# A decode layer on one core: where the hand-written section of all engines ends, and how w_down's loads are issued

## The chip, the core and the metric

One core of one Trainium2 chip runs the whole kernel. The metric is device time in microseconds, the median of the runs; a profiled execution stands beside it with a trace of every instruction and of every DMA packet. TensorE (PE), VectorE (DVE), ScalarE (ACT) and GpSimd (POOL) compute; SyncE (SP) issues nearly all loads. All loads share sixteen DMA engines.

## What is computed

One token goes through an attention block with a cached context of 65,536 positions and a gated feed-forward block, in bf16:

```python
x = A_x                                   # 1 x 1 x 1024
h = x + attention(layernorm(x), k_cache, v_cache, wq, wo)   # 32 query heads, 4 kv heads, Sk = 65536, Dh = 128
g = gelu(layernorm(h) @ w_gate)           # w_gate 1024 x 3584
u = layernorm(h) @ w_up                   # w_up   1024 x 3584
out = h + (g * u) @ w_down                # w_down 3584 x 1024
```

The caches are 134 MB and the weights 39 MB; each byte is read once and used for a single token.

## The kernel before

**Loads.** All weights and caches pass through `ring`, a buffer of four slots of 32 KB in each of 128 partitions. SP issues the loads in program order: wq, the K and V chunks in a loop over eight half-heads, wo in two halves, then `w_gate` (7168 KB, slots 0 and 1, issued when the last product with V has been taken out of them), `w_up` (7168 KB, slots 2 and 3, when wo has been used), and `w_down` in six pieces:

- wa, 4096 KB, into slot 0, and wb, 2048 KB, into slot 1, both once gate's matmuls are done with these slots;
- 768 KB into `w_end`, a buffer of its own outside of the ring, and
- the last 256 KB, also into `w_end`, in three loads over 57 odd partitions, 7 odd partitions and the 64 even ones.

**Order of the work.** Two mechanisms set it. `Flow` is a list written out by hand: each `op` or `dma` names what it reads and writes, and `Flow.issue` (lines 83 to 118) emits the instructions in list order with the least waits on the kernel's own semaphores. Its output stands in a *critical section* (line 612): to the framework's scheduler the section is one unit, which begins through SP and ends in a join. At the end every engine that took part drains and signals; SP waits for all signals and then signals the end, and only behind that come instructions that depend on the section. A second section (line 658) holds the first part of the down projection. Outside of sections the scheduler places the semaphores itself, from what each instruction reads and writes; `manual_schedule` makes it keep TensorE's instructions in the order written, and `keep_in_program_order` does so for single instructions of SP.

**The feed-forward part.** `ffn_in` loads a matrix, multiplies it in eight steps (`wide_rows`, four matmuls side by side into each of the banks 0 and 1) and brings the rows into columns by two DVE transposes. For gate that is followed by the gelu on DVE and ACT (`t1`, `th`, `hg`, `gl`). The residual h is put into the output's accumulators `d_ps` (bank 2) and `d_odd` (bank 7) by eight matmuls against `hb`, which POOL fills by a memset and a product; POOL also clears `actz`, into whose column the product of gate and up is written. Then the down projection: `stay_busy(4)` runs four filler matmuls, `down_wide` takes wa's part in 32 matmuls of 512 columns, ACT copies the result to `e_sb`, `stay_busy(3)` fills, `add_wide` folds it into the accumulators, and `down` takes wb's 8 rows and `w_end`'s 3 + 1 rows in 8 matmuls of 128 columns each. DVE and ACT take the two halves of the accumulators to bf16, and SP stores them.

**Names and lines.** Everything that `Flow.issue` emits has line 105 in the profile (waits of its own: 101). L172: the first load. L612: the first section's begin and end. L621: the loads into `w_end`. L631: `down`. L638: `stay_busy`. L646: `down_wide`. L653: `add_wide`. L658: the second section's begin and end. L665: `e_sb`. L673: waits on `w_end`'s loads. L677 to L679: the output. In the profile `ktb` stands for whatever lies over that buffer at the time, `hb`, `actz`, the transposed rows and `at_r` among them.

In the kernel before, the first section ends behind the product of gate and up:

```python
    u_r = ffn_in(B_w_up, "u_r", 2, 0)
    op("dve", "tensor_tensor", r=["u_r0", "u_r1", "gl", "actz"], w=["actz"], out=actz[:, :, AZ], in0=u_r, in1=gl[:], op=ALU.mult)
```

Of the kernel before, what the change touches and what calls it, by code (L numbers as in the profile page):

```python
# [8 lines left out]
ACT = mybir.ActivationFunctionType  # L9
ALU = mybir.AluOpType  # L10
# [108 lines left out]
def kernel(  # L119
# [13 lines left out]
    nc = tc.nc  # L133
    P = 128
    D = A_x.shape[-1]
# [4 lines left out]
    F = B_w_gate.shape[1]  # L140
    DC = D // P
    FC = F // P
# [39 lines left out]
    def sb(name, shape, dtype=F32):  # L182
        return const.tile(shape, dtype, name=name)
# [22 lines left out]
    def slot(i, n=1):  # L206
        return ring[:, i * CW:(i + n) * CW]
# [5 lines left out]
    act_go = tc.alloc_semaphore("to_act")  # L213
    STEPS = 4
    k_sem = [tc.alloc_semaphore("k_landed_%d" % i) for i in range(DCH)]
    end_sem = [tc.alloc_semaphore("end_landed_%d" % i) for i in range(2)]


    XU = 32
# [333 lines left out]
    def f_blocks(w_row):  # L553

        blocks = []
        for o, n in zip((0, P * FA), FW):
            blocks += [w_row[:, o + q * n:o + (q + 1) * n] for q in range(4)]
        return blocks

    def ffn_in(wmat, key, s0, b0):  # L560
        banks = [bank[b0 + i][:, 0:n] for i, n in enumerate(FW)]
        bkeys = ["B%d" % (b0 + i) for i in range(2)]
# [3 lines left out]
        for ci in range(DC):  # L566
            wide_rows(banks, bkeys, hz, "xz", ci, f_blocks(wv[:, ci, :]), rk, ci == 0, ci == DC - 1)
        return rows_to_columns(banks, bkeys, key, "p (j e) -> p e j", j=32)

    g_sb = ffn_in(B_w_gate, "g_r", 0, 0)  # L570
    t1 = sb("t1", [P, FC])
    op("dve", "tensor_tensor", r=["g_r0", "g_r1"], w=["t1"], out=t1[:], in0=g_sb, in1=g_sb, op=ALU.mult)
    op("dve", "tensor_scalar", r=["t1"], w=["t1"], out=t1[:], in0=t1[:], scalar1=0.044715, scalar2=1.0, op0=ALU.mult, op1=ALU.add)
    op("dve", "tensor_tensor", r=["t1", "g_r0", "g_r1"], w=["t1"], out=t1[:], in0=t1[:], in1=g_sb, op=ALU.mult)
    th = sb("th", [P, FC])
    op("act", "activation", r=["t1"], w=["th"], out=th[:], in_=t1[:], func=ACT.Tanh, scale=0.7978845608028654)
    hg = sb("hg", [P, FC])
    op("dve", "tensor_scalar", r=["g_r0", "g_r1"], w=["hg"], out=hg[:], in0=g_sb, scalar1=0.5, scalar2=None, op0=ALU.mult)
    gl = sb("gl", [P, FC])
    op("dve", "scalar_tensor_tensor", r=["th", "hg"], w=["gl"], out=gl[:], in0=th[:], scalar=1.0, in1=hg[:], op0=ALU.add, op1=ALU.mult)  # L580


    OR = 8
    OB = D // OR
    orow = [30, 94, 31, 95, 32, 96, 33, 97]
    d_ps = bank[2][:, 0:OB]
    op("dve", "memset", w=["B2"], ap=d_ps, constant=0.0)
    hb = over(10240, [DC, P])
    op("pool", "memset", w=["hb"], ap=hb, constant=0.0)
    op("pool", "tensor_tensor", r=["h_col", "o_of"], w=["hb"], out=hb.rearrange("p j (b m) -> p j m b", b=2)[:, :, orow[0]:orow[0] + OR // 2, :],  # L590
       in0=h_col[:].unsqueeze(2).unsqueeze(3).to_broadcast([P, DC, OR // 2, 2]),
       in1=o_of[:].rearrange("p (a b) -> p a b", b=2).unsqueeze(1).to_broadcast([P, DC, OR // 2, 2]), op=ALU.mult)
    for j in range(DC):
        op("pe", "matmul", r=["hb", "sel16"], w=["B2"], out=d_ps[:, j:OB:DC], lhsT=hb[:, j, :], rhs=sel16[:],
           start=False, stop=False, skip_group_check=True)
    d_odd = bank[7][:, 0:OB]
    op("dve", "tensor_copy", r=["B2"], w=["B7"], out=d_odd[64:P, :], in_=d_ps[64:P, :])

    AZ = 31
    actz = over(16384, [FC, 2 * AZ + 2], BF16)  # L600
    op("pool", "memset", w=["actz"], ap=actz, constant=0.0)
    u_r = ffn_in(B_w_up, "u_r", 2, 0)
    op("dve", "tensor_tensor", r=["u_r0", "u_r1", "gl", "actz"], w=["actz"], out=actz[:, :, AZ], in0=u_r, in1=gl[:], op=ALU.mult)

    wa = slot(0)[:, 0:FA * D].rearrange("p (e n) -> p e n", e=FA)
    wb = slot(1)[:, 0:FB * D].rearrange("p (e n) -> p e n", e=FB)
    parts = [(wa, 0, FA, f.dma("sp", wa, B_w_down[0:P * FA, :].rearrange("(p e) n -> p e n", p=P), after=["R0"], inc=(r_sem[0], 16)), r_sem[0])]
    e0 = 0
    w_body = wb_src[:, e0:FB - FZ, :]
    part = wb[:, e0:FB - FZ, :]  # L610
    parts.append((part, FA + e0, FB - FZ - e0, f.dma("sp", part, w_body, after=["R1"], inc=(r_sem[1], 16)), r_sem[1]))
    with tc.tile_critical(no_gpsimd_drain=True):  # L612
        f.issue()

    ends = []
    odd = [57, 7]
    for i, (e1, e2, rows) in enumerate(((FB - FZ, FB - 1, [slice(0, P)]),
                                        (FB - 1, FB, [slice(1, 2 * odd[0], 2), slice(2 * odd[0] + 1, P, 2), slice(0, P, 2)]))):
        loads = []
        for p in rows:  # L620
            d = nc.sync.dma_start(out=w_end[p, e1 - FB + FZ:e2 - FB + FZ, :], in_=wb_src[p, e1:e2, :])  # L621
            d.then_inc(end_sem[i], 16)
            tc.no_tile_sem_insts.add(d.ins.name)
            tc.keep_in_program_order(d)
            loads.append(d)
        ends.append((loads, e1, e2))

    def down(a_row, w_row, landed=()):
        for j in (0, 4, 1, 5, 2, 6, 3, 7):
            q, m = divmod(orow[j], 32)  # L630
            mm = nc.tensor.matmul((d_ps, d_odd)[q // 2][32 * q:32 * q + 32, :], lhsT=a_row[:, AZ - m:AZ - m + 32], rhs=w_row[:, j * OB:(j + 1) * OB],  # L631
                             start=False, stop=False, skip_group_check=True, tile_position=(0, 32 * q))
            for d in landed:
                tc.declare_no_dep(mm.ins, d.ins, query=mybir.DependencyQuery.ANY, reason="TensorE waits for the load's own semaphore ahead of it")

    def stay_busy(n):
        for i in range(n):
# [5 lines left out]
    def down_wide(a_row, w_row, e, n):  # L643
        for h in range(DS):
            q = 2 * (e % 2) + h
            mm = nc.tensor.matmul(e_ps[32 * q:32 * q + 32, :], lhsT=a_row[:, AZ:AZ + 32], rhs=w_row[:, h * NB:(h + 1) * NB],  # L646
                             start=(e < 2), stop=(e >= n - 2), tile_position=(0, 32 * q))
        return mm

    def add_wide():  # L650
        for c in range(C4):
# [4 lines left out]
    (w_rows, a0, n, at, sem), (w_rows2, a2, n2, at2, sem2) = parts  # L656
    ctx.enter_context(tc.manual_schedule(engines={mybir.EngineType.PE}))
    with tc.tile_critical(no_gpsimd_drain=True):  # L658
        stay_busy(4)
        nc.tensor.wait_ge(sem, at)  # L660
        for e in range(n):
            mm = down_wide(actz[:, a0 + e, :], w_rows[:, e, :], e, n)
        mm.then_inc(s_step, 1)
        nc.scalar.wait_ge(s_step, STEPS * NT2 + 1)
        nc.scalar.copy(out=e_sb[:], in_=e_ps[:]).then_inc(from_act, 1)  # L665
        stay_busy(3)
        nc.tensor.wait_ge(from_act, 1)
        add_wide()
        nc.tensor.wait_ge(sem2, at2)
        for e in range(n2):  # L670
            down(actz[:, a2 + e, :], w_rows2[:, e, :])
    for i, (d, e1, e2) in enumerate(ends):
        nc.tensor.wait_ge(end_sem[i], 16 * len(d))  # L673
        for e in range(e1, e2):
            down(actz[:, FA + e, :], w_end[:, e - FB + FZ, :], d)
    h2 = sb("h2", [P, 2, OB], BF16)
    nc.vector.tensor_copy(out=h2[0:64, 0, :], in_=d_ps[0:64, :])  # L677
    nc.scalar.copy(out=h2[0:64, 1, :], in_=d_odd[64:P, :])  # L678
# [31 lines left out]
```

## Time and profile before

| | |
|---|---|
| median of 3 runs | 409.45 us (409.44, 409.45, 410.83) |
| profiled execution | 409.35 us |
| its span, first to last instruction | 407.6 us |
| bytes read | 173.02 MB, 424 GB/s over the span |
| busy share of PE, DVE, ACT, POOL | 55%, 49%, 10%, 4% |
| mean granted PE clock | 0.812 of full speed |
| `w_gate` landed, its matmuls done | 370.67, 375.36 us |
| `w_up` landed, its matmuls done | 387.62, 392.30 us |
| wa, wb landed | 397.32, 402.21 us |
| last 32 matmuls of the down projection | 404.44 to 405.07 us |

Times in the trace are counted from the first instruction, so that the span's end is 407.6. A landing is the time at which the last of the sixteen DMA engines has posted its completion of that load; single engines can be far ahead of it. Waits are put down to what released them: "SPq L612 <- DVEq L612" is SP standing in the join until DVE had drained. The granted clock is the share of full speed that TensorE was allowed. Line and operation names of DMA issues (DMA_DIRECT2D) stand on the queue that issues them, SPq.

### The profile page before, as it was taken

How to read it: one execution, taken by the hardware profiler on the slowest of the kernel's cores; microseconds unless marked ns; L12 is line 12 of the kernel's file. 1: busy time of each engine (PE TensorE's matmuls, PEld its weight loads, DVE VectorE, ACT ScalarE, POOL GpSimd, SP SyncE). 2: the span in 40 equal slices, each digit the busy share in tenths (PEclk: the TensorE clock that was granted, in tenths of full speed). 3: DMA queues.
4: the chain of work that ended last, by engine and by line, in shares of the span. 5: the costliest groups of instructions: out<-in, count | busy, mean ns of one | idle time of the engine just before them, and what ended most of it. 6: DMA issues, size and time to landing. Idle time of an engine off the chain costs nothing. (4 is left out here: it accounts for less than half of the span.)

```text
span 407.6 us, 3816 instructions
## 1 busy us (share of the span) xinstructions
PE 225.4 (55%) x1557; PEld 99.4 (24%) x1558; DVE 201.1 (49%) x160; ACT 40.2 (10%) x143; POOL 14.7 (4%) x25
## 2 busy tenths in 40 slices
PE   0432854674677458715971785468467745624156
PEld 0110322231232133203320332223123223222123
DVE  4126860894089328734763686088508940121010
ACT  1000003000300120030003000300030003000000
POOL 4010000001000000010000001000000000030000
PEclk9995996899569778978796889589956986866688
DMA  8999999999999999999998999999999999999995
GB/s 360 412 447 426 447 428 412 460 418 435 431 460 418 412 447 473 412 415 415 489 431 383 444 421 450 418 463 412 415 453 463 418 412 418 461 450 435 394 413 219
DMA packets 4967, 173.10 MB, mean 425 GB/s; under 512 B 606, under 2 KB 610, under 8 KB 866
## 3 DMA queue, kind: packets, MB, share of 16 engines
q1 hardware_dynamic: 4914, 173.02, 98.6%
q8 instruction: 4, 0.07, 0.1%
q10 hardware_dynamic: 48, 0.00, 0.0%
q14 instruction: 1, 0.01, 0.0%
HBM read 173.02 MB, written 0.00 MB: 424 GB/s over the span
## 5 line engine op out<-in xcount | busy, mean ns | idle before, releaser
L105 DVE STREAM_TRANSPOSE ktb<-ring 128x4096 f32<-128x4096 f32 x32 | 141.1, 4418 | 74.9 <-DMA ring<-in_A_k_cache_dram 74.9
L455 PE MATMUL bank<-ktb,qs 128*128 128x512 bf16 x512 | 131.3, 416 | 53.6 <-PEq L441 53.6
L455 PEld LDWEIGHTS bank<-ktb,qs 128*128 128x128 bf16 x512 | 51.3, 103 | 130.3 <-issue 84.1
L467 PE MATMUL bank<-ring,pt 128*32 128x512 bf16 x512 | 43.4, 513 | 38.0 <-PEq L441 38.0
L414 ACT ACTIVATE pt<-sc,nb 128x256 bf16<-128x256 f32 x64 | 31.5, 494 | 258.0 <-ACTq L410 258.0
L105 DVE STREAM_TRANSPOSE sc<-bank 128x512 f32<-128x512 f32 x32 | 22.3, 696 | 37.6 <-PE bank L455 37.6
L467 PEld LDWEIGHTS bank<-ring,pt 128*32 128x32 bf16 x512 | 18.4, 124 | 59.7 <-issue 55.4
L105 PE MATMUL bank<-ring,xz 128*32 128x512 bf16 (+1 forms) x192 | 16.0, 506 | 24.6 <-DMA ring<-in_B_w_gate_dram 9.9
L105 DVE STREAM_TRANSPOSE ktb<-bank 128x512 f32<-128x512 f32 (+1 forms) x6 | 3.7, 651 | 37.0 <-PE bank L105 37.0
L105 DVE TENSOR_REDUCE mx<-sc 128x8 f32<-128x2048 f32 x8 | 18.3, 2286 | 0.3
L459 PE MATMUL bank<-ident_f,mx 128*8 128x128 f32 x8 | 2.6, 321 | 25.8 <-PEq L441 25.8
L105 PEld LDWEIGHTS bank<-ring,xz 128*32 128x32 bf16 x192 | 6.3, 126 | 33.2 <-issue 15.9
L105 POOL COPY qs<-qsel 128x512 bf16<-128x512 bf16 x4 | 5.3, 1325 | 234.4 <-PE bank L455 219.0
L476 PE MATMUL bank<-sel,acc_sb 128*128 128x8 f32 x64 | 8.2, 255 | 6.9 <-PEq L441 6.9
L414 ACT ACTIVATION_READ_ACCUMULATOR pt<-sc,nb x64 | 12.0, 187 | 0.0
L476 PEld LDWEIGHTS bank<-sel,acc_sb 128*128 128x128 f32 x64 | 7.7, 191 | 10.6 <-issue 10.6
L418 ACT COPY acc_sb<-bank 128x512 f32<-128x512 f32 x8 | 4.7, 585 | 46.8 <-ACTq L417 46.8
L459 PEld LDWEIGHTS bank<-ident_f,mx 128*8 128x8 f32 x8 | 0.7, 83 | 29.5 <-issue 29.5
L461 PE MATMUL bank<-diag,ones_f 8*128 8x8 f32 x16 | 3.7, 300 | 5.7 <-PEq L441 5.7
L105 POOL MEMSET ktb<- 128x1024 bf16 (+2 forms) x3 | 3.5, 1164 | 77.3 <-PE bank L455 77.3
L105 PE MATMUL bank<-ring,ktb 128*32 128x512 bf16 x64 | 5.6, 506 | 1.2 <-POOL ktb L105 0.7
L677 DVE CAST h<-bank 64x128 bf16<-64x128 f32 x1 | 0.3, 283 | 11.3 <-PE bank L631 11.3
(97 smaller groups left out, 59.5 us busy)
## 6 DMA issues: line engine op xcount, KB each, us to landing
ring<-in_A_k_cache_dram SPq DMA_DIRECT2D x16, 4096.0 KB, 24.9
ring<-in_A_wq_dram SPq DMA_DIRECT2D x2, 4096.0 KB, 16.6
ring<-in_A_wo_dram SPq DMA_DIRECT2D x2, 4096.0 KB, 24.0
ring<-in_B_w_gate_dram SPq DMA_DIRECT2D x1, 7168.0 KB, 23.9
ring<-in_B_w_up_dram SPq DMA_DIRECT2D x1, 7168.0 KB, 31.8
ring<-in_B_w_down_dram SPq DMA_DIRECT2D x1, 4096.0 KB, 21.9
ring<-in_B_w_down_dram SPq DMA_DIRECT2D x1, 2048.0 KB, 26.5
w_end<-in_B_w_down_dram SPq DMA_DIRECT2D x1, 768.0 KB, 27.9
```

What stands on the lines that cost most here:

```text
L105: ins = getattr(self.eng[e], o["call"])(**o["kw"])
L414: m = nc.scalar.activation(out=pt[:].rearrange("p c n h s -> p (c n) h s")[:, :, r, :], in_=sc[:].rearrange("p c n h s -> p (c n) h s")[:, ...
L418: nc.scalar.copy(out=acc_sb[:], in_=acc[:]).then_inc(from_act, 1)
L455: m = nc.tensor.matmul(bank[c][:], lhsT=qs[:, jt].rearrange("p s c -> p (s c)")[:, s * P:(s + 1) * P], rhs=mv[:, :, J, :, u], start=(s == ...
L459: nc.tensor.transpose(out=mxT_ps, in_=mx1[:], identity=ident_f[:]).then_inc(s_step, 1)
L461: nc.tensor.matmul(bc_ps, lhsT=ones_f[0:rep, :], rhs=diag[:], start=True, stop=True).then_inc(s_step, 1)
L467: m = nc.tensor.matmul(acc[32 * q:32 * q + 32, :], lhsT=pt[:, c, n, :, :].rearrange("p h s -> p (h s)"), rhs=v_sb[:, c, :, n, :], start=(c ...
L476: m = nc.tensor.matmul(o_ps, lhsT=acc_sb[:, u * Dh:(u + 1) * Dh], rhs=sel[:, u:SQ:NS], start=(u == 0), stop=(u == NS - 1))
L677: nc.vector.tensor_copy(out=h2[0:64, 0, :], in_=d_ps[0:64, :])
```

## The change

1. The list in `Flow`, and with it the first section, ends with gate's matmuls and the issue of `w_up`'s load. The function `ffn_in` becomes `ffn_load` (the load alone), and gate's matmuls are written out behind it.
2. What follows is outside of sections. The region of TensorE's written order begins here. The six loads of `w_down` come first, from one list, each kept in program order, with a semaphore for each of the four pieces (`end_sem`, 4 instead of 2). They belong to a group whose fence is a no-operation of TensorE: instructions behind it don't wait for these loads by the framework's semaphores, and TensorE waits for the pieces' own ones.
3. POOL's filling of `hb` and clearing of `actz`, DVE's memset, transposes and gelu, ACT's tanh and TensorE's hb matmuls are plain instructions now, with semaphores placed by the framework; POOL's three are behind the section's end instead of within it.
4. The wait for `w_up` stands in a small section of its own, of TensorE alone. Up's matmuls, the transposes (`columns`) and the product into `actz` follow outside.
5. The second section is taken away: `stay_busy(4)`, wa's wait and matmuls, `e_sb`, `stay_busy(2)` instead of 3, `add_wide` and a loop over the other three pieces follow outside of sections.

```diff
-    end_sem = [tc.alloc_semaphore("end_landed_%d" % i) for i in range(2)]
+    end_sem = [tc.alloc_semaphore("end_landed_%d" % i) for i in range(4)]
...
+    f_banks = [bank[i][:, 0:n] for i, n in enumerate(FW)]
+    gate_w, rk = ffn_load(B_w_gate, 0)
+    for ci in range(DC):
+        wide_rows(f_banks, ["B0", "B1"], hz, "xz", ci, f_blocks(gate_w[:, ci, :]), rk, ci == 0, ci == DC - 1)
+    up_w, _ = ffn_load(B_w_up, 2)
+    with tc.tile_critical(no_gpsimd_drain=True):
+        f.issue()
+
+    ctx.enter_context(tc.manual_schedule(engines={mybir.EngineType.PE}))
...
+    loads = [(wa, B_w_down[0:P * FA, :].rearrange("(p e) n -> p e n", p=P)), (wb[:, 0:FM, :], wb_src[:, 0:FM, :]),
+             (w_end[:, 0:FZ - 1, :], wb_src[:, FM:FB - 1, :]), (w_end[:, FZ - 1:FZ, :], wb_src[:, FB - 1:FB, :])]
+    odd = [57, 7]
+    shares = [[slice(0, P)]] * 3 + [[slice(1, 2 * odd[0], 2), slice(2 * odd[0] + 1, P, 2), slice(0, P, 2)]]
+    for (dst, src), sem, share in zip(loads, end_sem, shares):
+        for p in share:
+            d = nc.sync.dma_start(out=dst[p], in_=src[p])
+            d.then_inc(sem, 16)
+            tc.no_tile_sem_insts.add(d.ins.name)
+            tc.add_to_no_dep_group("loads", d.ins)
+            tc.keep_in_program_order(d)
+    waits_itself = nc.tensor.nop()
+    tc.declare_fence(waits_itself.ins, group="loads")
...
-    op("pool", "memset", w=["hb"], ap=hb, constant=0.0)
...
+    nc.gpsimd.memset(hb, 0.0)
...
+    nc.gpsimd.memset(actz, 0.0)
+
+    def columns(r):
+        o = 0
+        for ps, n in zip(f_banks, FW):
+            nc.vector.transpose(out=r[:, o:o + n].rearrange("p (e j) -> p e j", j=32), in_=ps.rearrange("p (j e) -> p e j", j=32))
+            o += n
+        return r[:, 0:o:32]
...
+    with tc.tile_critical(no_gpsimd_drain=True):
+        nc.tensor.wait_ge(r_sem[2], f.landed[r_sem[2].name])
+    for ci in range(DC):
+        for t, w in enumerate(f_blocks(up_w[:, ci, :])):
+            q = t % 4
+            nc.tensor.matmul(f_banks[t // 4][32 * q:32 * q + 32, :], lhsT=hz[:, ci, :], rhs=w, start=(ci == 0), stop=(ci == DC - 1),
+                             tile_position=(0, 32 * q))
+    u_r = columns(over(28672, [sum(FW)]))
+    nc.vector.tensor_tensor(out=actz[:, :, AZ], in0=u_r, in1=gl[:], op=ALU.mult)
...
-    with tc.tile_critical(no_gpsimd_drain=True):
-        stay_busy(4)
-        nc.tensor.wait_ge(sem, at)
...
-        stay_busy(3)
-        nc.tensor.wait_ge(from_act, 1)
-        add_wide()
...
+    stay_busy(4)
+    nc.tensor.wait_ge(end_sem[0], 16)
+    for e in range(FA):
+        down_wide(actz[:, e, :], wa[:, e, :], e, FA)
+    nc.scalar.copy(out=e_sb[:], in_=e_ps[:])
+    stay_busy(2)
+    add_wide()
+    e = FA
+    for (dst, _), sem, share in list(zip(loads, end_sem, shares))[1:]:
+        nc.tensor.wait_ge(sem, 16 * len(share))
+        for i in range(dst.shape[1]):
+            down(actz[:, e, :], dst[:, i, :])
+            e += 1
```

More of the change, by code (lines that the diff above doesn't have):

```diff
@@ L558, in f_blocks, with ffn_load @@
         return blocks
-    def ffn_in(wmat, key, s0, b0):
-        banks = [bank[b0 + i][:, 0:n] for i, n in enumerate(FW)]
-        bkeys = ["B%d" % (b0 + i) for i in range(2)]
+    def ffn_load(wmat, s0):
         rk = ["R%d" % s0, "R%d" % (s0 + 1)]
@@ L565, in ffn_in @@
         f.dma("sp", wv, wmat.rearrange("(p c) n -> p c n", p=P), w=rk, sem=r_sem[s0], wait=[(s_step, STEPS * NT2)])
[L566 to L578, printed above, removed]
@@ L579 @@
-    gl = sb("gl", [P, FC])
-    op("dve", "scalar_tensor_tensor", r=["th", "hg"], w=["gl"], out=gl[:], in0=th[:], scalar=1.0, in1=hg[:], op0=ALU.add, op1=ALU.mult)
+        return wv, rk
+    f_banks = [bank[i][:, 0:n] for i, n in enumerate(FW)]
[5 more added lines that the diff above has]
+        f.issue()
@@ new lines @@
+    ctx.enter_context(tc.manual_schedule(engines={mybir.EngineType.PE}))
+    wa = slot(0)[:, 0:FA * D].rearrange("p (e n) -> p e n", e=FA)
+    wb = slot(1)[:, 0:FB * D].rearrange("p (e n) -> p e n", e=FB)
+    wb_src = B_w_down[P * FA:F, :].rearrange("(p e) n -> p e n", p=P)
+    FM = FB - FZ
+    loads = [(wa, B_w_down[0:P * FA, :].rearrange("(p e) n -> p e n", p=P)), (wb[:, 0:FM, :], wb_src[:, 0:FM, :]),
+             (w_end[:, 0:FZ - 1, :], wb_src[:, FM:FB - 1, :]), (w_end[:, FZ - 1:FZ, :], wb_src[:, FB - 1:FB, :])]
@@ L586 @@
     d_ps = bank[2][:, 0:OB]
-    op("dve", "memset", w=["B2"], ap=d_ps, constant=0.0)
     hb = over(10240, [DC, P])
-    op("pool", "memset", w=["hb"], ap=hb, constant=0.0)
-    op("pool", "tensor_tensor", r=["h_col", "o_of"], w=["hb"], out=hb.rearrange("p j (b m) -> p j m b", b=2)[:, :, orow[0]:orow[0] + OR // 2, :],
-       in0=h_col[:].unsqueeze(2).unsqueeze(3).to_broadcast([P, DC, OR // 2, 2]),
-       in1=o_of[:].rearrange("p (a b) -> p a b", b=2).unsqueeze(1).to_broadcast([P, DC, OR // 2, 2]), op=ALU.mult)
@@ L593 @@
[L593 to L597, printed above, removed]
     AZ = 31
     actz = over(16384, [FC, 2 * AZ + 2], BF16)
-    op("pool", "memset", w=["actz"], ap=actz, constant=0.0)
-    u_r = ffn_in(B_w_up, "u_r", 2, 0)
-    op("dve", "tensor_tensor", r=["u_r0", "u_r1", "gl", "actz"], w=["actz"], out=actz[:, :, AZ], in0=u_r, in1=gl[:], op=ALU.mult)
@@ L605 @@
[L605 to L626, printed above, removed]
@@ L628, in down @@
-    def down(a_row, w_row, landed=()):
+    nc.gpsimd.memset(hb, 0.0)
+    nc.gpsimd.tensor_tensor(out=hb.rearrange("p j (b m) -> p j m b", b=2)[:, :, orow[0]:orow[0] + OR // 2, :],
+                            in0=h_col[:].unsqueeze(2).unsqueeze(3).to_broadcast([P, DC, OR // 2, 2]),
+                            in1=o_of[:].rearrange("p (a b) -> p a b", b=2).unsqueeze(1).to_broadcast([P, DC, OR // 2, 2]), op=ALU.mult)
+    nc.gpsimd.memset(actz, 0.0)
[5 more added lines that the diff above has]
+        return r[:, 0:o:32]
@@ new lines @@
+    nc.vector.memset(d_ps, 0.0)
+    g_sb = columns(over(28672, [sum(FW)]))
+    t1, th, hg, gl = [sb(n, [P, FC]) for n in ("t1", "th", "hg", "gl")]
+    nc.vector.tensor_tensor(out=t1[:], in0=g_sb, in1=g_sb, op=ALU.mult)
+    nc.vector.tensor_scalar(out=t1[:], in0=t1[:], scalar1=0.044715, scalar2=1.0, op0=ALU.mult, op1=ALU.add)
+    nc.vector.tensor_tensor(out=t1[:], in0=t1[:], in1=g_sb, op=ALU.mult)
+    nc.scalar.activation(out=th[:], in_=t1[:], func=ACT.Tanh, scale=0.7978845608028654)
+    nc.vector.tensor_scalar(out=hg[:], in0=g_sb, scalar1=0.5, scalar2=None, op0=ALU.mult)
@@ new lines @@
+    nc.vector.scalar_tensor_tensor(out=gl[:], in0=th[:], scalar=1.0, in1=hg[:], op0=ALU.add, op1=ALU.mult)
+    for j in range(DC):
+        nc.tensor.matmul(d_ps[:, j:OB:DC], lhsT=hb[:, j, :], rhs=sel16[:], start=False, stop=False, skip_group_check=True)
+    d_odd = bank[7][:, 0:OB]
+    nc.vector.tensor_copy(out=d_odd[64:P, :], in_=d_ps[64:P, :])
+    with tc.tile_critical(no_gpsimd_drain=True):
+        nc.tensor.wait_ge(r_sem[2], f.landed[r_sem[2].name])
[4 more added lines that the diff above has]
+                             tile_position=(0, 32 * q))
@@ L629, in down @@
+    u_r = columns(over(28672, [sum(FW)]))
+    nc.vector.tensor_tensor(out=actz[:, :, AZ], in0=u_r, in1=gl[:], op=ALU.mult)
+    def down(a_row, w_row):
         for j in (0, 4, 1, 5, 2, 6, 3, 7):
             q, m = divmod(orow[j], 32)
-            mm = nc.tensor.matmul((d_ps, d_odd)[q // 2][32 * q:32 * q + 32, :], lhsT=a_row[:, AZ - m:AZ - m + 32], rhs=w_row[:, j * OB:(j + 1) * OB],
+            nc.tensor.matmul((d_ps, d_odd)[q // 2][32 * q:32 * q + 32, :], lhsT=a_row[:, AZ - m:AZ - m + 32], rhs=w_row[:, j * OB:(j + 1) * OB],
@@ L632, in down @@
                              start=False, stop=False, skip_group_check=True, tile_position=(0, 32 * q))
-            for d in landed:
-                tc.declare_no_dep(mm.ins, d.ins, query=mybir.DependencyQuery.ANY, reason="TensorE waits for the load's own semaphore ahead of it")
     def stay_busy(n):
@@ L645, in down_wide @@
             q = 2 * (e % 2) + h
-            mm = nc.tensor.matmul(e_ps[32 * q:32 * q + 32, :], lhsT=a_row[:, AZ:AZ + 32], rhs=w_row[:, h * NB:(h + 1) * NB],
+            nc.tensor.matmul(e_ps[32 * q:32 * q + 32, :], lhsT=a_row[:, AZ:AZ + 32], rhs=w_row[:, h * NB:(h + 1) * NB],
                              start=(e < 2), stop=(e >= n - 2), tile_position=(0, 32 * q))
-        return mm
     def add_wide():
@@ L654, in add_wide @@
                              start=False, stop=False, skip_group_check=True, tile_position=(0, 64 * h))
-    (w_rows, a0, n, at, sem), (w_rows2, a2, n2, at2, sem2) = parts
-    ctx.enter_context(tc.manual_schedule(engines={mybir.EngineType.PE}))
-    with tc.tile_critical(no_gpsimd_drain=True):
-        stay_busy(4)
-        nc.tensor.wait_ge(sem, at)
[L661 to L665, printed above, removed]
-        stay_busy(3)
-        nc.tensor.wait_ge(from_act, 1)
-        add_wide()
[L669 to L675, printed above, removed]
+    stay_busy(4)
[11 more added lines that the diff above has]
+            e += 1
     h2 = sb("h2", [P, 2, OB], BF16)
```

## The prediction

> **What bounds the kernel now.** I read the page's queue table first, then the chain that ended last, then SP's own instructions and waits, then a table of busy time by stage for the last 20 us. The queue table and the last stretches of that table (columns: stretch, its us, busy us and count of PE, PEld, DVE, ACT, POOL, then granted PE clock, DMA share, GB/s) say that the DMA engines are the bound until 404 us:
>
> ```profile
> q1 hardware_dynamic: 4914, 173.02, 98.6%
> q8 instruction: 4, 0.07, 0.1%
> ...
> 388.00:390.60 2.60, 2.60 (x32) 1.10 (x28) 0.00 (x0) 0.00 (x0) 0.00 (x0) 0.50 0.99 429
> 394.00:396.60 2.60, 0.00 (x0) 0.00 (x0) 0.00 (x0) 0.00 (x0) 0.00 (x0) 1.00 0.83 353
> 397.40:400.80 3.40, 3.40 (x32) 1.09 (x32) 0.00 (x0) 0.00 (x0) 0.00 (x0) 0.50 1.01 427
> 402.00:404.30 2.30, 1.57 (x72) 1.22 (x72) 0.00 (x0) 0.00 (x0) 0.00 (x0) 1.00 0.45 159
> ```
>
> The loads' queue q1 takes 98.6% of sixteen engines' span. In the trace's packet records each engine's packets follow one another without a pause from 1.9 us on, apart from the instruction queue's four packets of 16 KB, at 31.8, 353.8, 376.75 and 401.49 us, each of which holds one engine for some 1.03 us. The share falls only after 402 us, when most engines have run dry and a few have not. The chain's end (start, us, what):
>
> ```profile
> 370.80 4.56 PE bank L105 x63
> ...
> 376.43 27.87 DMA w_end<-in_B_w_down_dram
> 404.30 0.14 issue
> 404.44 0.68 PE bank L631 x32
> 405.12 0.02 issue
> 405.14 0.26 ACT h L678
> ```
>
> The chain goes through a load that took 27.87 us from issue to landing, but it stood behind 13 MB of earlier loads nearly all that time; its issue is not what it waited for. After the landing only 0.8 us of TensorE, 0.3 us of copies, the store and the closing barrier follow. SP's queue and its longest wait in the tail:
>
> ```profile
> 355.83 0.33 SPq L105 DMA_DIRECT2D ring<-in_B_w_up_dram  x1
> 375.38 0.80 SPq L105 DMA_DIRECT2D ring<-in_B_w_down_dram  x2
> 376.43 19.83 SPq L621 DMA_DIRECT2D w_end<-in_B_w_down_dram  x4
> ...
> SPq L612 <- DVEq L612: 17.1, 1, 17.1
> ```
>
> The first three of w_down's loads (4096, 2048 and 768 KB) are issued at 375.38, 375.75 and 376.43 us. SP then stands 17.1 us in the join at the first section's end (L612, DVE's drain ends at 393.80), and the last three, 256 KB in all, go out at 394.04, 394.94 and 395.74 us. They still come in time: the queue has work until 402. So the one thing here that waits visibly costs nothing.
>
> **The change, part by part.**
>
> *Section's end, before the loads.* Now wa (L105) is issued as soon as gate's last matmul signals, at 375.38. In the new kernel it stands behind the join. Price, from the old join: PE's drain ended 0.07 us after its last matmul (392.30, 392.37), and from the last drain's end to the next load's issue took 0.24 us (393.80, 394.04). All other engines' drains are long past, since the section has nothing behind gate's matmuls. So wa at 375.36 + 0.07 + 0.24, about 375.7: 0.3 us later. Cover: `w_up`'s load, whose first engine posts its completion at 385.7. A load's first packet moves 1.1 us after its issue (first load: issue 0.78, packet 1.86), so the deadline is 384.6, and 8.9 us are spare. Cost 0. Without the cover it would be 0.3.
>
> *Six loads in a row.* Issue times by the old rows: 0.80 for wa and wb together, 0.33, then 0.85, 0.75 and 0.52 for the three shares of the last row: done by about 379.0 (3.3 us). Three of them move 15 us forward, past the join and nothing else on SP. Order and bytes on each DMA engine stay, each engine is busy from here to its last packet in either case, so no packet moves earlier: 0.
>
> *POOL's three steps* move from 361.7-364.5 to behind the join, and DVE's and ACT's steps stay behind gate's matmuls:
>
> ```profile
> 361.68 0.95 POOL L105 MEMSET ktb<- 128x1024 f32 x1
> 362.71 0.31 POOL L105 TENSOR_TENSOR ktb<-h_col,o_of 128x64 f32<-128x64 f32 x1
> 362.95 1.59 POOL L105 MEMSET ktb<- 128x1792 bf16 x1
> ```
>
> From 375.7: `hb` ready at 377.1 (0.95 + 0.31 and hand-overs), `actz` cleared at 378.6. TensorE's 8 hb matmuls (1.96 us) then end at 379.1, against 379.8 now, where a DVE memset at 377.6 held them. DVE's transposes and gelu (2.5 us in all) end by 378.5, its copy of the odd rows (0.31) by 379.5. `w_up` lands at 387.62, so 8 us of waiting hide all of this; without that cover its 3.4 us from join to last hb matmul would count.
>
> *A section for the wait on `w_up`.* TensorE enters through SP, behind the six loads: at 379.0 plus 0.37 (old second section, SP's start 396.32 to TensorE's first weight load 396.69), long before the landing. Leaving costs between 0.12 (old join, drain's end 403.60 to 403.72) and 0.4 us on the path of up's matmuls. They start at 387.8 to 388.1 instead of 387.66, end by 392.7, and `actz` is written by 394.2 (DVE's two transposes and product, 1.57 us). wa lands at 397.32: 3.1 us spare. Cost 0.
>
> *The second section goes, `stay_busy` becomes 4 + 2.* The four run right after up's matmuls instead of at 396.7, so the wide matmuls start on wa's landing, 397.35 instead of 397.83. At their old 3.4 us they end at 400.8; e_sb's copy (0.58), two fillers and add_wide (0.66) end by 402.2, wb lands at 402.21, its 64 matmuls (1.08) end at 403.4 instead of 403.57. The join at 403.7 is gone too. All of this gain (0.2 to 0.3 us) lies in front of the landing at 404.30 and is worth 0 there.
>
> *What no row shows: where the instruction fetches fall.* Counted by engine, the completions of gate's load show 3 late engines of 16 (370.1 to 370.7, the rest by 369.24), those of wa 4, those of the 768 KB load 5 (403.8 to 404.3, the rest by 402.8); each fetch in between added one. The new program has a few other instructions on TensorE, so the last fetch can move. Bounds: if it strikes an engine that is late already, +1.03 us; if it comes behind the engine's last packet, up to -1.0. I take 0, as nearly the same number of instructions lies in front of it. The Trainium skill ("Runtime: NRT & Kernel Launch", Instruction fetch mechanics) calls the cost of such a block's refill mostly hidden; by it this term would be 0 without bounds. The trace disagrees so far as a DMA engine is what is late.
>
> **Sum.** 0 on the path: span 407.6, and 1.75 us around it, as in the profiled execution (409.35). The median of the runs shown is 0.1 above it. I forecast **409.4**, by itself within 408.3 to 410.5 (one fetch either way, rounded up for the scatter seen: one of the three runs was 410.83).
>
> **Rivals.**
>
> *SP takes the new section ahead of the loads.* If SP stands in the section of the `w_up` wait first, the loads go out only after 387.62 + 0.2, first packet at 388.9. Twelve engines ran dry by 386.2 and would lose 2.7 or more (402.8 becomes 405.5 to 405.9), the late four 1.3 to 1.9 (404.3 becomes 405.6). End 1.4 later: **410.8**; if the section is left only behind up's matmuls, 392.5, it is 402.8 + 7.4 = 410.2 instead of 404.3, some 415. It decides as soon as wa's issue passes 384.6. For it: SP leads every section, and stood 17.1 us in one. Against: the hb matmuls, 3.4 us of work, lie between, and the loads are ready at the join. Chance 0.10, a third of it at the far end.
>
> *The tail runs cold.* The granted clock was 0.50 at 397.4-400.8, after a stretch without matmuls, and the fillers move away from that point. Should it stay low past 400.8, take the clock's price from up's matmuls: 32 in 2.60 us at 0.50, 36 in 1.70 at 1.00, a ratio of 1.72. wb's 64 would end at 402.3 + 1.86 = 404.2, just hidden, and the last 32 take 1.08 instead of 0.63: **409.8**. Against: TensorE is then busy for 3.4 us ahead of 400.8, after which the old run was granted full clock. Chance 0.08. The Trainium skill ("TensorE: Matmul & The Clock Gate", Part 1) has the clock halved after an idle window of some 3.4 us and restored after a busy one; fillers moved 4 us ahead leave such a gap, so it speaks against the move.
>
> *The fetch moves.* **408.4** (0.09) or **410.4** (0.09), as bounded above.
>
> *TensorE stalls for code in the tail*, behind one of the new section's ends: a 16 KB packet of 1.03 us, behind one load packet of 1.22 us and 1.1 us of start, 3.3 us; if that falls on 404.3, **412.7**. No such stall is seen before. Chance 0.05.
>
> *All late engines catch up*, since the joins and branches change and the loads spread: the end falls from 404.3 to 402.8, then TensorE binds at 403.4: **408.5**, floor 407.9. Chance 0.04. Nothing in the change takes a byte away.
>
> *The change does not do what it says* (loads interleaved with other engines' steps): as long as wa leaves before 384.6 it is the forecast again.
>
> **How the numbers follow.** The forecast itself has 0.55. A difference of 0.5% (407.4, 411.5) is about what a measurement of this kernel can tell from no change. Faster than that lies below every case's price and needs scatter as well: 0.06. Slower: the far end of the first rival, the stall, and half of the rest of the first rival with scatter, rounded up for what I do not see: 0.18. Within: 0.76. The range reaches from the floor, 407.9, to 412.0, short of the stall and the first rival's far end.
>
> **What would show it.** In the changed kernel's trace: wa's issue at 375.6 to 376.0 and all six issues before 380; DMA share near 1 from 380 to 402; up's matmuls at 387.8 to 388.1; the wide ones at wa's landing; a landing of the last load at 403.3 to 405.3, and TensorE's last 32 matmuls right behind it. I am wrong if a gap in the DMA share opens near 386, if the last matmuls start well after the last landing, or if the landings have more than five late engines.

## The result, and the profile after

The changed kernel takes **409.42 us** (median of 22 runs, 409.33 to 409.79); the kernel before, run beside it, takes 410.48 us (median of 22 runs, 409.35 to 411.32). The ratio is 0.9979, with a 95% interval of 0.9972 to 0.9987. The number forecast was 409.4 and the class forecast was "within 0.5%"; both hold. Yet the interval lies below 1: the kernel is 0.2% faster, and the forecast said "0". The shortest runs are the same to 0.02 us. What is gone is the scatter: the kernel before spreads over some 2 us, the changed one over less than half a microsecond. The three runs shown at first (409.44, 409.45, 410.83) and the profiled execution (409.35) happened to lie mostly at the lower end of it.

The queue table of the changed kernel, with the share of sixteen DMA engines' span in the last column, and the chain that ended last (start, us, what):

```profile
q1 hardware_dynamic: 4914, 173.02, 98.5%
```

```profile
375.90 0.33 SPq L585
...
376.75 27.80 DMA w_end<-in_B_w_down_dram
404.55 0.04 issue
404.60 0.69 PE bank L640 x32
```

The chain is the old one: the 768 KB load, issued at 376.75, lands at 404.55, and the last 32 matmuls follow at once (the last row's three loads land at 404.84, while these matmuls run). The DMA engines still set this execution's end (409.53 us, span 407.8). SP's own instructions (start, us, engine line operation, tiles) show what the change did to its queue:

```profile
375.90 0.80 SPq L585 DMA_DIRECT2D ring<-in_B_w_down_dram  x2
376.75 2.68 SPq L585 DMA_DIRECT2D w_end<-in_B_w_down_dram  x4
405.63 0.31 SPq L678 DMA_DIRECT2D out_dram<-h  x1
```

All six loads go out between 375.90 and 379.43, and SP has nothing more to do until the store. TensorE's tail, in the same form with its idle time and what ended it in brackets:

```profile
388.45 6.15 PE L632 MATMUL bank<-ring,xz 128*32 128x512 bf16 x64 [7.79 <-PEq L627]
394.76 0.81 PE L645 MATMUL bank<-qs 128*128 128x512 bf16 x3 [0.16 <-issue]
397.65 3.44 PE L653 MATMUL bank<-ring,ktb 128*32 128x512 bf16 x32 [2.08 <-DMA ring<-in_B_w_down_dram]
...
402.55 1.08 PE L640 MATMUL bank<-ring,ktb 128*32 128x128 bf16 x64
404.60 0.63 PE L640 MATMUL bank<-w_end,ktb 128*32 128x128 bf16 x32 [0.97 <-DMA w_end<-in_B_w_down_dram]
```

The wide matmuls (L653) wait 2.08 us for wa and start right behind its landing at 397.52. This is the line to compare. In the profiled execution of the kernel before, with the same columns, the wait for SP's queue stood ahead of the fillers, and the wide matmuls did not wait for a load at all:

```profile
387.66 4.64 PE L105 MATMUL bank<-ring,xz 128*32 128x512 bf16 x64 [7.88 <-DMA ring<-in_B_w_up_dram]
396.92 0.98 PE L638 MATMUL bank<-qs 128*128 128x512 bf16 x3 [4.62 <-SPq L658]
397.83 3.38 PE L646 MATMUL bank<-ring,ktb 128*32 128x512 bf16 x32
```

There the fillers were released by SP's queue (L658, the second section's entry) after 4.62 us of idling, and the wide matmuls started 0.5 us behind wa's landing at 397.32. In that execution it mattered little. How much it matters in others is what the experiments found.

### The profile page after: what moved, and what is told of

It is laid out like the page before. It is cut to its first block, busy times and chain, and to the rows that moved or that the text cites. A ratio compares the mean times of both kernels' runs of the same rounds, so it can differ in the third digit from the quotient of the medians.

```text
span 407.8 us, 3811 instructions
## 1 busy us (share of the span) xinstructions
PE 226.7 (56%) x1556; PEld 100.1 (25%) x1557; DVE 201.1 (49%) x160; ACT 40.3 (10%) x143; POOL 14.8 (4%) x25
## 5 line engine op out<-in xcount | busy, mean ns | idle before, releaser
L105 PE MATMUL bank<-ring,xz 128*32 128x512 bf16 (+1 forms) x128 | 11.7, 538 | 16.9 <-DMA ring<-in_B_w_gate_dram 10.0
L632 PE MATMUL bank<-ring,xz 128*32 128x512 bf16 (+1 forms) x64 | 6.1, 577 | 7.8 <-PEq L627 7.8
L105 PEld LDWEIGHTS bank<-ring,xz 128*32 128x32 bf16 x128 | 4.4, 128 | 23.2 <-issue 14.3
L609 DVE STREAM_TRANSPOSE ktb<-bank 128x512 f32<-128x512 f32 (+1 forms) x4 | 2.3, 618 | 13.3 <-PE bank L632 13.3
L105 DVE STREAM_TRANSPOSE ktb<-bank 128x512 f32<-128x512 f32 x2 | 1.3, 696 | 12.6 <-PE bank L105 12.6
```

The costliest lines, as they stand in the source:

```text
L105: ins = getattr(self.eng[e], o["call"])(**o["kw"])
L609: nc.vector.transpose(out=r[:, o:o + n].rearrange("p (e j) -> p e j", j=32), in_=ps.rearrange("p (j e) -> p e j", j=32))
L632: nc.tensor.matmul(f_banks[t // 4][32 * q:32 * q + 32, :], lhsT=hz[:, ci, :], rhs=w, start=(ci == 0), stop=(ci == DC - 1), tile_position=( ...
```

## The experiments

Three theories stood at the start. **A**: TensorE's tail starts late, since the fillers and the wide matmuls may start only when SP has opened the second section; how late it ends depends on the granted clock. **B**: the last row's loads were too late in some runs, so that the landing itself moved. **C**: an instruction packet strikes a DMA engine that is late already. A was narrowed on the way: the second section alone does not do it (the run with the section put back), and what remained are the three late issues that stand on SP between the join and that section's entry. Ratios are to the kernel before, run on the same chip in the same series (410.4, 410.02 and 410.22 us in the three series).

**The kernel before once more** (no edit), to see where its scatter lies.

> The kernel before, unchanged, for the spread of its runs (409.35 to 411.32 us, against 409.33 to 409.79 of the changed one) and a second trace. Theory A, the tail of TensorE: in the slower runs the down projection ends after the last landing, since the fillers and the wide matmuls start only when SP has opened the second section and the granted clock happens to be low then; a slower profiled run would show wb's 64 matmuls at half clock or the last 32 starting well after the last landing. Theory B, the last three loads issued at 394 us land late: last landing later than 404.7 with the others as before. Theory C, an instruction fetch strikes a DMA engine that is late already: one engine 1 us later than the rest of the late ones. Runs between 409.3 and 411.3 by all three; ratio 1.000.

Measured: 410.62 us (409.43 to 411.52, 12 runs), 1.0008 [0.9995, 1.0020]. Its profile fell on an execution of 411.17 us, span 409.5. TensorE's tail there:

```profile
387.66 6.10 PE L105 MATMUL bank<-ring,xz 128*32 128x512 bf16 x64 [5.32 <-DMA ring<-in_B_w_up_dram]
398.45 1.49 PE L638 MATMUL bank<-qs 128*128 128x512 bf16 x3 [4.69 <-SPq L658]
399.87 3.60 PE L646 MATMUL bank<-ring,ktb 128*32 128x512 bf16 x32
...
404.93 1.08 PE L631 MATMUL bank<-ring,ktb 128*32 128x128 bf16 x64
406.26 0.63 PE L631 MATMUL bank<-w_end,ktb 128*32 128x128 bf16 x32 [0.25 <-SPq L658]
```

and its table by stage (stretch, its us, busy us and count of PE, PEld, DVE, ACT, POOL, then granted PE clock, DMA share, GB/s):

```profile
397.40:400.80 3.40, 2.35 (x15) 0.83 (x20) 0.00 (x0) 0.00 (x0) 0.00 (x0) 0.50 0.99 418
400.80:402.30 1.50, 1.50 (x20) 0.53 (x16) 0.00 (x0) 0.00 (x0) 0.00 (x0) 0.50 0.97 385
402.30:404.30 2.00, 2.00 (x15) 0.39 (x7) 0.00 (x0) 0.58 (x1) 0.00 (x0) 0.62 0.38 131
404.30:405.20 0.90, 0.90 (x29) 0.69 (x32) 0.00 (x0) 0.00 (x0) 0.00 (x0) 1.00 0.00 0
```

The landings are as before: wa at 397.33, the 768 KB at 404.38, the last row at 404.71. Theories B and C have no place here: no landing is later than in the faster execution (409.35) by more than 0.1 us. But up's matmuls ran at half clock to their end (6.10 us instead of 4.64; the clock came back at 393.57, in the faster execution at 390.60), the product was made at 395.12, the join ended at 395.33, the three loads were issued from 395.39 to 397.61, the section was entered at 397.67, and the wide matmuls began at 399.87, 2.5 us behind the landing. In the last stretch the DMA share is 0 and TensorE is busy throughout: here TensorE sets the end. Its last 32 matmuls start 1.9 us after the 768 KB landed and 1.55 us after the last row did (406.26 against 404.38 and 404.71). The chain that ended last (start, us, what) says the same; no DMA stands in it from the second section's entry (L658) on:

```profile
397.73 0.02 SPq L658
397.75 0.70 issue
398.45 1.49 PE bank L638 x3
399.94 3.57 PE bank L646 x32
...
405.66 0.39 PEldq L658
...
406.26 0.68 PE bank L631 x32
```

The three issues hold SP for 2.28 us of this (395.39 to 397.67). By an estimate from these rows, the last 32 matmuls without them could start at 406.26 - 2.28, about 404.0, which is ahead of the 768 KB's landing.

Each run's mean granted clock comes with its time, so the scatter can be sorted by it. The runs of the kernel before in the three series, 92 different pairs of time and clock, and beside them the changed kernel's 22:

```
mean clock    before: runs, lowest - highest us     after: runs, lowest - highest us
0.779-0.783    9    410.29 - 410.69                  1    409.62
0.787-0.789   23    409.69 - 410.98                  2    409.78 - 409.79
0.791-0.795   25    409.59 - 410.88                  4    409.34 - 409.77
0.796          2    410.68 - 410.81                  0
0.798-0.799    4    409.49 - 409.87                  2    409.38 - 409.41
0.803          6    409.41 - 409.75                  1    409.41
0.807          3    409.36 - 409.41                  5    409.36 - 409.53
0.808          9    411.01 - 411.52                  1    409.70
0.812-0.824   11    409.31 - 411.07                  6    409.33 - 409.46
```

The middle run of the kernel before lies at 410.5 us for a clock of 0.783, at 409.4 for 0.807 and at 411.1 for 0.808, and within some rows the runs lie 1 us and more apart; the changed kernel stays within half a microsecond throughout. The amount of half clock is not what decides: runs at 0.807 have spans of 407.7 us and runs at 0.808 of some 409.4 us, so that both lose the same time to it (0.193 of the one and 0.192 of the other, 78.7 and 78.6 us). The steps of 0.004 fit one stretch of half clock each: the low stretch of the execution above lasted from 379.91 to 393.57, 13.66 us, and the next from 396.98 to 403.81, 6.83 us, four and two times 3.415 us; 3.415 us at half clock are 0.0042 of 407.8 us. The Trainium skill ("TensorE: Matmul & The Clock Gate", Part 1) has a window of 3413 ns that runs freely and does not restart with the kernel; these stretches agree, and their edges lie elsewhere in the two profiled executions of the same kernel (a low stretch starts at 380.36 in one and at 379.91 in the other). That the time of the kernel before goes with the place of these stretches is what the two profiles show, 409.35 against 411.17 us. The table fits it but does not show for each single run where they lay.

**The second section put back into the changed kernel**, with all loads left where the change has them (abridged; the steps inside are moved into the section).

```diff
+    with tc.tile_critical(no_gpsimd_drain=True):
         stay_busy(4)
         nc.tensor.wait_ge(end_sem[0], 16)
         (wide matmuls, e_sb's copy, two fillers, add_wide, wb's 64)
```

> The changed kernel with the second section put back around fillers, wa's, add_wide's and wb's part (two fillers in the middle as in the changed kernel). Loads are still issued in one go near 376. Theory A: the spread of the kernel before comes back, median 410 to 410.6 us, runs up to 411. Theories B and C: no second group, runs from 409.3 to 409.8 like the changed kernel.

Measured: 409.78 us (409.67 to 409.99, 12 runs), 0.9989 [0.9979, 0.9998]. The section was entered at 395.21 and the wide matmuls started at 397.40, at wa's landing. The span is 407.7, as without the section (407.8), and the scatter does not come back: theory A as it stood at the start had expected it here. The 0.35 us that its runs lie above the changed kernel's stand outside the span: time less span is 2.04 to 2.11 us in them, and 1.66 to 1.81 in the runs of both kernels. Why is open; a kernel below with three sections too has 1.69 to 1.78, so their number alone is not it. On the path that sets the end the section itself is worth nothing.

**The last row's loads issued late**, behind a wait of SP for wa's landing.

```diff
+        if len(share) > 1:
+            tc.keep_in_program_order(nc.sync.wait_ge(end_sem[0], 16))
         for p in share:
```

> The changed kernel with SP waiting for wa's landing (about 397.5) before it issues the three loads of the last row, later still than the 394 to 396 us of the kernel before. Theory B: the spread comes back, median 410 or more. Theories A and C and the forecast's reading (the DMA engines have work until 402, issue time is worth nothing): as the changed kernel, 409.3 to 409.8 us.

Measured: 409.48 us (409.35 to 410.02, 12 runs), 0.9983 [0.9973, 0.9993]. The three loads were issued from 397.34 to 399.55, later than in either kernel, and still landed at 404.67. So their issue time is worth nothing to the DMA engines, as forecast, and theory B falls. What it cost must lie on SP.

**The first rival of the prediction, made true**: SP waits for `w_up`'s landing before the six loads.

```diff
+    with tc.tile_critical(no_gpsimd_drain=True):
+        nc.sync.wait_ge(r_sem[2], f.landed[r_sem[2].name])
     for (dst, src), sem, share in zip(loads, end_sem, shares):
```

> The changed kernel with a small section in which SP waits for w_up's landing ahead of the six loads: the first rival of the prediction made true. By its price the DMA engines run dry from 386 to 389, the last landing is at 405.6 to 405.9 and the time is 410.8 us, 1.4 above the changed kernel. If the loads' issue were hidden in any case, 409.4; if TensorE's tail were the bound, less than 1.4 more.

Measured: 413.69 us (413.59 to 414.08, 4 runs), 1.0086 [1.0064, 1.0107]. wa was issued at 387.80. The table by stage, same columns as above (a packet counts in the stretch in which it starts):

```profile
384.00:386.00 2.00, 0.00 (x0) 0.00 (x0) 0.00 (x0) 0.00 (x0) 0.00 (x0) 0.50 0.27 115
386.00:387.00 1.00, 0.00 (x0) 0.00 (x0) 0.00 (x0) 0.00 (x0) 0.00 (x0) 0.50 0.00 0
387.00:388.00 1.00, 0.00 (x0) 0.00 (x0) 0.00 (x0) 0.00 (x0) 0.00 (x0) 0.50 0.00 0
388.00:389.00 1.00, 0.00 (x0) 0.00 (x0) 0.00 (x0) 0.00 (x0) 0.00 (x0) 0.50 1.30 360
```

The gap that the prediction named as a sign of this rival is there, but 4.3 us are lost against the changed kernel (413.69 and 409.42) and not 1.4. In the two profiles 3.64 us of it are the landing of the 768 KB (408.19 against 404.55), and 0.42 are the last 32 matmuls, which fell on half clock (1.05 us instead of 0.63). The engines run dry from 385.2 on, half a microsecond and more before the completions that I had counted from. And after the pause all sixteen are level again: fifteen finish the 768 KB between 406.29 and 406.75, and one, probably the one that an instruction packet of 0.93 us held at 403.40, finishes at 408.19. I had let the lateness of a few engines hide the gap; the gap levels them, and the next fetch makes one late again on top.

**No fillers at all**, for the rival of the cold tail.

```diff
-    stay_busy(4)
     nc.tensor.wait_ge(end_sem[0], 16)
...
-    stay_busy(2)
     add_wide()
```

> The changed kernel without any filler matmuls. If the forecast's reading holds (TensorE waits for landings, the clock is restored by the wide matmuls themselves), 409.3 to 409.9 us. Rival of the prediction, the cold tail: wb's 64 matmuls at half clock end at 404.2 and the last 32 take 1.05 us, 409.9 to 410.2 us.

Measured: 409.45 us (409.29 to 410.24, 10 runs), 0.9987 [0.9976, 0.9998]. The median is the changed kernel's: without any fillers the tail costs nothing that these runs show. In the profiled execution the wide matmuls ran from 397.40 for 3.57 us and wb's 64 started at 402.24. One run in ten lies at 410.24, above all of the changed kernel's; whether that is a cold tail no profile of it shows.

**The kernel before without its first four fillers**, which stand behind the section's entry.

```diff
     with tc.tile_critical(no_gpsimd_drain=True):
-        stay_busy(4)
         nc.tensor.wait_ge(sem, at)
```

> The kernel before without the four filler matmuls ahead of wa's wait. Theory A: the fillers stand between SP's late release and the wide matmuls, 1.0 us at full clock and 1.5 at half; without them the wide ones start at 398.0 in the slow runs, and the median falls from 410.5 to 409.5-409.9 us, highest run 410.6. Rival: the joins behind wb's matmuls or the clock in the last matmuls cost the time: median stays 410.3 or more.

Measured: 409.61 us (409.34 to 410.17, 11 runs), 0.9989 [0.9978, 1.0000]. The wide matmuls start at 397.40 and the last 32 at 404.55. Taking the fillers out from between SP's entry and the wide matmuls (0.98 and 1.49 us in the two profiles of the kernel before) removes much of the scatter, without moving a load.

**POOL's three steps back into the first section**, ahead of its join, which now waits for POOL too (abridged; the three plain instructions further down go).

```diff
-    with tc.tile_critical(no_gpsimd_drain=True):
+    op("pool", "memset", w=["hb"], ap=hb, constant=0.0)
+    op("pool", "tensor_tensor", ...)
+    op("pool", "memset", w=["actz"], ap=actz, constant=0.0)
+    with tc.tile_critical():
         f.issue()
```

> The changed kernel with POOL's three steps for hb and actz put back into the first section (which now drains POOL too). If POOL's memset is what stretches two DVE steps on 28 columns to 1.1 and 1.0 us behind gate's matmuls, these go back to 0.18 us and the hb matmuls start at 377.7 to 378.2 instead of 378.7. Time as the changed kernel, 409.3 to 409.8 us, since w_up lands 8 us later.

Measured: 409.40 us (409.31 to 409.90, 10 runs), 0.9992 [0.9983, 1.0001]. The hb matmuls start at 375.91 instead of 378.71, and the time is that of the changed kernel: the stretch before `w_up`'s landing hides POOL's steps wherever they stand.

**The three late issues alone, put into the changed kernel.** A first attempt wrote them behind the product without a wait of SP's own:

```diff
+    with tc.tile_critical(no_gpsimd_drain=True):
+        nc.vector.tensor_tensor(...)      (the product)
+    for p in shares[3]:
+        d = nc.sync.dma_start(out=loads[3][0][p], in_=loads[3][1][p])
+    (second section as above)
```

> The changed kernel with the second section put back and, as in the kernel before, the three loads of the last row between a join that waits for the product into actz and that section's entry, on SP (some 2.2 us of issues). Theory A, made precise: what stretches the kernel before is that TensorE may start its fillers only when SP has issued these three loads, so that the wide matmuls begin 0.5 to 2.5 us after wa's landing, depending on the granted clock. The spread comes back: median 410.2 to 411.2 us, highest 411.5 or more, wide matmuls at 398 to 400.5. Rival: the section alone, wherever SP enters it, costs 0.35 us: 409.7 to 410.0 us as in the run with the section put back.

Measured: 409.80 us (409.63 to 409.90, 11 runs), 0.9995 [0.9986, 1.0004]. SP issued the loads early all the same, so they were not between the sections, and this says nothing about theory A. It is one more kernel with a late entry (397.0) and wide matmuls at 398.88, 1.4 us behind the landing, whose slack still holds: span 407.8, with 2.06 us around it. The second attempt puts the issues into the product's section, behind a wait for the product (abridged):

```diff
+    with tc.tile_critical(no_gpsimd_drain=True):
+        nc.vector.tensor_tensor(...).then_inc(made, 1)      (the product)
+        nc.sync.wait_ge(made, 1)
+        for p in shares[3]:
+            nc.sync.dma_start(out=loads[3][0][p], in_=loads[3][1][p]).then_inc(end_sem[3], 16)
+    (second section as above, w_end's matmuls inside it)
```

> The changed kernel with the second section put back and the three loads of the last row issued in a section of their own behind the product into actz, so that SP does have these issues (2.2 us) between that product and the second section's entry; in the earlier attempt SP had issued them long before, and the entry came at 397.0. w_end's matmuls stand in the second section. Theory A: entry at 398.3 or later, wide matmuls at 399.5 to 401, the last 32 matmuls 1 to 2.5 us after the last landing: median 410.5 to 412 us. Rival, the section alone: 409.7 to 410.0 as before.

Measured: 411.39 us (410.04 to 412.23, 12 runs), 1.0025 [1.0012, 1.0038]. SP's issues and TensorE's tail, in the form used above:

```profile
395.71 2.23 SPq L640 DMA_DIRECT2D w_end<-in_B_w_down_dram  x3
```

```profile
398.94 1.89 PE L650 MATMUL bank<-qs 128*128 128x512 bf16 x4 [5.10 <-SPq L668]
400.75 3.12 PE L658 MATMUL bank<-ring,ktb 128*32 128x512 bf16 x32
...
406.06 0.62 PE L645 MATMUL bank<-w_end,ktb 128*32 128x128 bf16 x32
```

With 2.23 us of issues between the product and the entry (and 0.6 us more for the end of the product's section, 397.94 to 398.56), the wide matmuls start at 400.75, the last 32 run without a wait 1.3 us after the last landing (404.79), and the scatter is back, with the same pattern over the clock: 410.98 and 411.33 at 0.783, 410.04 at 0.803, 412.14 and 412.23 at 0.809. Of what it lies above the kernel before (410.22), 0.37 us stand outside the span, as in the two kernels above (2.04 to 2.18 around it); the spans themselves run from 408.0 to 410.1, where the two kernels above with the second section have 407.7 and 407.8 in their profiles.

**The three late issues alone, taken out of the kernel before**: w_end's four loads go into the hand-written list behind wb's, w_end's matmuls into the second section (so that this section's join, worth 0.25 us ahead of the last 32 matmuls in the profile of 411.17 us, comes behind them), and all else stays (abridged).

```diff
         for p in rows:
-            d = nc.sync.dma_start(out=w_end[p, ...], in_=wb_src[p, e1:e2, :])
-            d.then_inc(end_sem[i], 16)
+            f.dma("sp", w_end[p, ...], wb_src[p, e1:e2, :], inc=(end_sem[i], 16))
+    with tc.tile_critical(no_gpsimd_drain=True):
+        f.issue()
```

> The kernel before with one part of the change alone: the four loads into w_end stand in the hand-written list right behind wb's, inside the long first section, so that all six go out near 376-379 us and SP has nothing to issue between the first section's join and the second section's entry; both sections stay (w_end's matmuls stand in the second one, so the casts wait for its join, 0.1 to 0.2 us). Theory A: TensorE is released 2.2 us earlier, the fillers are over when wa lands, and the spread goes: median 409.5 to 409.9 us, highest 410.2. Rival: the long first section or the clock alone makes the spread: median 410.2 or more, runs up to 411.

Measured: 409.50 us (409.37 to 409.73, 12 runs), 0.9979 [0.9969, 0.9988]. SP's and TensorE's rows:

```profile
376.16 0.80 SPq L105 DMA_DIRECT2D ring<-in_B_w_down_dram  x2
377.00 3.48 SPq L105 DMA_DIRECT2D w_end<-in_B_w_down_dram  x4
```

```profile
395.18 1.59 PE L632 MATMUL bank<-qs 128*128 128x512 bf16 x4 [2.11 <-SPq L652]
397.43 2.63 PE L640 MATMUL bank<-ring,ktb 128*32 128x512 bf16 x32 [0.66 <-DMA ring<-in_B_w_down_dram]
...
404.48 0.63 PE L625 MATMUL bank<-w_end,ktb 128*32 128x128 bf16 x32 [1.06 <-DMA w_end<-in_B_w_down_dram]
```

The fillers start 2.11 us after TensorE's last work instead of 4.6 to 4.7, the wide matmuls wait for wa and not for SP, and the scatter is gone. This one part brings the whole ratio of the change, with both sections, all fillers and POOL's steps as they were.

## Why the prediction was right in its number and wrong in a step

**The bound.** Right. The 768 KB load's issue is not what it waits for; the last landing was forecast at 403.3 to 405.3, and this one came at 404.55 (the last row's at 404.84), with five late engines (403.93 to 404.55) and the rest by 402.8. TensorE's last matmuls follow it by 0.05 us. The floor of both kernels is this landing, 409.33 and 409.35 us.

**"Section's end, before the loads".** Right. wa was forecast at about 375.7 and left at 375.90; no gap opened near 386. The step's deadline of 384.6 was 0.4 us too late: the engines are dry from 385.2, and in the experiment the first packet moved 0.96 us after wa's issue (388.76 and 387.80). The price behind it was further off: 4.3 us for 1.4.

**"Six loads in a row ... 0".** This is the step that failed. For the DMA engines the zero is right, and the run with the last row's loads at 397.34 shows it. The step looked at what the three loads bring and not at what stood behind them on SP's queue: "past the join and nothing else on SP" leaves out the second section's entry, which is SP's next work. "So the one thing here that waits visibly costs nothing" was said of the loads and is false of their queue. The join ends when the product is made (at 394.0 in one execution and 395.3 in the other), the three issues take 2.2 us, and only then does TensorE get in, 0.5 us behind wa's landing in one execution and 2.5 us in another. The slack that absorbs it was 0.73 us in the execution that I read (wb's matmuls ended at 403.57, the landing was at 404.30): enough there, not enough when up's matmuls, the fillers and the wide matmuls run at half clock. The two kernels that move the three issues alone show it from both sides: out of the old kernel, 0.9979; into the new one with its second section, from 0.9989 to 1.0025.

**The baseline.** The sum was made against one execution at 409.35, and "scatter" stood in the range as something that the change leaves alone. It was a property of the kernel before, and the edit removes it. That the number came out at 409.4 is right for its reason, the landing, but in part luck in its start: from an execution like the one of 411.17 us, a sum of zeros would have given 411.2.

**"POOL's three steps".** The class is right, the times are not. The forecast had `hb` ready at 377.1 and its matmuls done by 379.1; they ended at 380.67, since POOL ran both memsets ahead of the product (done at 378.66). DVE's steps from `t1` to `gl` took 1.99 us beside them, and 1.15 with POOL's steps in the first section. Hidden all the same, as moving the steps back showed.

**"A section for the wait on w_up".** The way in was wrong. This section has TensorE alone in it, and no SP instruction stands at its line (L627): TensorE entered by itself at 378.79, while SP was still issuing until 379.43. So the first rival's ground, that SP leads every section, does not hold for this one. The exit was put at up to 0.4 us: `w_up` landed at 387.80 and the matmuls began at 388.45, 0.65 us later and outside of the 387.8 to 388.1 that were named as a sign. They took 6.15 us at half clock, not 4.64, so `actz` was written at 395.9 and not 394.2. Of the 3.1 us forecast as spare 1.6 were left (to 397.52). The zero held, with less room than I gave it.

**"The second section goes".** It was worth "0.2 to 0.3 us" ahead of the landing and 0 at the end. Putting it back leaves the span where it was (407.7 and 407.8), so the zero held; the 0.35 us that this kernel's runs are longer lie outside the span, where the sum had put 1.75 us without asking what they hold.

**Fetch, stall and cold tail.** The last fetch fell at 401.19 instead of 401.49 and the 768 KB's landing moved by 0.25 us; neither bound of 1.03 was reached. No stall for code shows. The tail of the changed kernel had full clock from 402.3 on:

```profile
391.00:394.00 3.00, 3.00 (x36) 1.43 (x32) 0.00 (x0) 0.00 (x0) 0.00 (x0) 0.50 0.99 426
397.40:400.80 3.40, 3.15 (x32) 1.32 (x32) 0.00 (x0) 0.00 (x0) 0.00 (x0) 0.57 0.98 414
402.30:404.30 2.00, 1.21 (x68) 0.90 (x64) 0.00 (x0) 0.00 (x0) 0.00 (x0) 1.00 0.46 158
```

The half clock that the rival feared came, but at 391 to 394 and at 397.4 to 400.8 (granted clock 0.50 and 0.57, third column from the right), where the loads cover it.

What stays open: in which runs exactly the windows fell how, and what a kernel without the instruction packets' late engines would take; no kernel here tried that. Nothing that was run beats the changed kernel clearly; four of those with one part changed end at 409.40 to 409.50 as well.

## What to carry to other kernels

A DMA issue that may be late for its data can still be early in somebody's way: list what stands behind each instruction on its queue, entries of sections with several engines among them, before calling its wait free. Read the slack of the path that ends second, and ask whether it still holds when the matmuls ahead of it run at half clock; a path with 0.7 us to spare in one profile was the one that set the end in another, 1.8 us later. And run the old kernel often enough to see its spread before taking one execution as its time.

## What the runs showed that I had not expected

Two DVE steps took 1.10 and 1.00 us beside a memset of POOL, and 0.18 us each without it. The kernel after, POOL and then DVE, in the form of the timeline above:

```profile
376.78 1.59 POOL L604 MEMSET ktb<- 128x1792 bf16 x1
```

```profile
377.31 1.10 DVE L620 TENSOR_SCALAR hg<-ktb 128x28 f32<-128x28 f32 x1
377.42 1.00 DVE L617 TENSOR_SCALAR t<-t 128x28 f32<-128x28 f32 x1
```

and the kernel with POOL's steps in the first section:

```profile
377.06 0.18 DVE L624 TENSOR_SCALAR hg<-ktb 128x28 f32<-128x28 f32 x1
377.18 0.18 DVE L621 TENSOR_SCALAR t<-t 128x28 f32<-128x28 f32 x1
```

Both steps end at 378.4, when the memset does (378.37), which reads as if they waited it out rather than ran slowly. The Trainium skill ("GPSIMD Engine Reference", 8. Key points) says that the two engines share SBUF interfaces and that some kinds of DVE instruction contend for them; for these two TENSOR_SCALAR steps the rows agree. That section counts DVE instructions with two SBUF inputs among them; the tensor_tensor at 377.19 has two and ran beside the memset in 0.20 us, so here it was not held. Why not, no run shows.

Levelling the DMA engines does not make them fast: after the pause in the kernel with the loads behind `w_up`, one engine finished 1.4 to 1.9 us later than all others, and the end waited for that one.
